# Three attention output projections as 64-row pairs at the end of the gate/up stage

## The chip, the cores and the metric

The kernel runs on one core of a Trainium2 chip. The metric is device time in microseconds (us), the median of the runs shown. The engines are TensorE (PE in the profile, with its weight loads as PEld), VectorE (DVE), ScalarE (ACT), GpSimd (POOL) and SyncE (SP); SyncE and GpSimd issue nearly all DMAs.

## The reference

One block with adaptive layer norm, 2048 rows of 576 channels, bf16: attention over a dilated window of 8 keys with 32 heads of 18 channels, then a gated bilinear feed-forward part with 4608 hidden channels. Cut to what matters:

```python
h = layernorm(x) * (1 + ca) + sa
qkv = h @ wqkv
o = windowed_attention(qkv)          # 8 keys, 2 apart, softmax
x = x + ga * (o @ wo)                # the output projection
h = layernorm(x) * (1 + cb) + sb
x = x + gb * (((h @ w_gate) * (h @ w_up)) @ w_down)
```

`sa, ca, ga, sb, cb, gb` come from `silu(c) @ w_mod`.

## The kernel before, in words

The rows are cut into 8 chunks of 256 (`CH`), each with two tiles of 128 rows. The feed-forward part takes the chunks in five groups, `GROUPS = [[0], [1, 2], [3, 4], [5, 6], [7]]`. For each group there is a stage `gate_up` (36 tiles of 128 hidden channels) and a stage `down` (the 36 tiles back to 576 channels).

576 channels are four tiles of 128 and a rest of 64. In gate/up a `Pair` computes two outputs at once, each half matmul using 64 of the 128 rows of TensorE: 9 steps of 64 channels, one output on the low rows and the other on the high rows, then swapped. `Pair.first` issues 10 of the 18 half matmuls, `Pair.second` the 8 others, and the first part of the next pair goes between. Gate and up of a tile are such a pair (`wg_pair`, 512 columns), and so are the q, k and v projections of later chunks (`qk_pair`, `v_pair`), which are put between the gate/up pairs. For that the last 64 rows of their weights stand twice in SBUF, in partitions 0 to 63 and 64 to 127, and so do the last 64 channels of their input.

All engines' orders are written out by the program at build time (manual schedule). `timed` is a small planner: it goes through the gate/up items, takes the next extra pair when its mark is due, and lets threads of other pieces (attention of the next group's chunks, layer norms, DMAs) in when its estimate of VectorE's time allows. A piece is `(TensorE time, VectorE time, needs, mark, wait, call)`; the times are the author's estimates in us, and they fix the order alone: on the chip every instruction waits for its data by semaphores. `among` does the same with the items of a down stage.

Attention of the chunks of the next group runs during gate/up, mostly on VectorE: products (`b_p`), logits (`b_l`, transposed by DMA in `b_ltd`), softmax (`b_sm0`, `b_sm1`), values (`b_mul`, `b_add`). The value windows `vsh` (1152 KB for one 128-row tile) are loaded by GpSimd (`b_ld`) into two buffers. The last `b_add` of a tile writes the attention output `o_sb`, rows by channels, 640 wide, of which 64 are padding with zeros. `b_od` issues two transposed DMAs on SyncE (one for each 128 rows) from `o_sb` to `oT`, channels by rows. `o_sb` and `oT` exist once.

`b_w` is the output projection of 128 rows: 5 matmuls of 64 columns (`pwr`) and 5 of 512 (`pw`) over five tiles of channels with 128 rows each (the last one padded with zeros), then three VectorE instructions that multiply with `ga` and add the residual `x_r`, giving a tile of `x1`. Chunk 0 has a form of its own. For every other chunk, `b_w` runs among the matmuls of the down stage of the group before. In a down stage of groups 1 to 3, `out_of` makes a thread for the next group's first chunk: `b_w` twice, the second layer norm (`b_ln`, `b_norm`), its transposes (`b_td`) into `h2T`, and the modulation (`b_mod`); the second chunk's thread begins with its `b_od` after the first chunk's `x1`. For the first chunk `b_od` was issued during gate/up before.

Loads of gate and up weights (`wgu`, two times 512 KB for four tiles) are issued by SyncE into three buffers, those of the down weights (`wd`, 576 KB) by GpSimd; some go to spaces free at that time (`prod_t`, `vsh`, `hh`).

Of the kernel before, what the change touches and what calls it, by code (L numbers as in the profile page):

```python
# [39 lines left out]
GC = D // 4  # L40

GROUPS = [[0], [1, 2], [3, 4], [5, 6], [7]]


@with_exitstack
def kernel(
# [48 lines left out]
    def js(j):  # L95
        return slice(j * P, (j + 1) * P)
# [44 lines left out]
    def load_res(i):  # L141
        x_res[i] = xres.tile([P, ST, D], BF, name="x_r")
        nc.sync.dma_start(x_res[i][:], x_rows(i))
# [399 lines left out]
    def b_mul(i, j, w0, n=2):  # L543
# [2 lines left out]
        at = b["attn"][:, j, w0:w0 + n, None, :].to_broadcast([P, n, DH, H])  # L546
        nc.vector.tensor_tensor(v, v, at, ALU.mult)  # L547

    def b_add(i, j, s):
        b = bb[i]  # L550
        vsh = b["vsh"][j]
        if s < 2:
            d = slice(2 * s, 2 * s + 2)
            nc.vector.tensor_tensor(vsh[:, d], vsh[:, d], vsh[:, 4 + 2 * s:6 + 2 * s], ALU.add)
        else:
            nc.vector.tensor_tensor(vsh[:, 0:2], vsh[:, 0:2], vsh[:, 2:4], ALU.add)
            nc.vector.tensor_tensor(o_sb[:, j, 0:D].rearrange("p (d h) -> p d h", d=DH), vsh[:, 0], vsh[:, 1], ALU.add)  # L557

    def b_o(i):
        pA = ps([P, 4, CH], BF, "oT_pA")  # L560
# [77 lines left out]
    def b_od(i):  # L638
        for j in range(ST):
            nc.sync.dma_start_transpose(out=oT[:, :, js(j)], in_=o_sb[:, j, :])  # L640
# [18 lines left out]
    def b_norm(i):  # L659
        bb[i]["rsq"]()  # L660
        bb[i]["norm"]()
# [24 lines left out]
    def prods_of(i):  # L686
        r = []
        if i >= 3:
            r = [(0, 0.82, "", f"p{i}{v}", 1.0, lambda v=v: b_p(i, v)) for v in range(W)]
            return r + [(1.3, 0, f"p{i}7", f"l{i}", 1.2, lambda: b_l(i, 0, 2)), (0, 0, f"l{i}", f"t{i}4", 9.0 if i == 7 else 6.0, lambda: [b_ltd(i, w) for w in (0, 4)])]  # L690
        for w in (0, 4):
            r += [(0, 0.82, "", f"p{i}{v}", 1.0, lambda v=v: b_p(i, v)) for v in range(w, w + 4)]
            r += [(0.75, 0, f"p{i}{w + 3}", f"l{i}{w}", 1.0, lambda w=w: b_l(i, w)), (0, 0, f"l{i}{w}", f"t{i}{w}", 9.0 if i == 7 else 6.0, lambda w=w: b_ltd(i, w))]
        return r

    def softmax_of(i):
        b1 = lambda: b_sm1(i)
        if i in GROUPS[1]:
            def total():
                b = bb[i]  # L700
                ssum = small.tile([P, ST, H], F32, name="ssum")
                nc.vector.tensor_reduce(ssum[:], b["dd"][:].rearrange("p j w h -> p j h w"), axis=AX.X, op=ALU.add)
                nc.scalar.activation(ssum[:], ssum[:], ACTF.Ln)
                b["rs"] = small.tile([P, ST, H], F32, name="rs")
                nc.scalar.activation(b["rs"][:], ssum[:], ACTF.Exp, scale=-1.0)

            def shares():
                b = bb[i]
                b["attn"] = attnp.tile([P, ST, W, H], BF, name="attn")
                nc.vector.tensor_tensor(b["attn"][:], b.pop("dd")[:], b.pop("rs")[:, :, None, :].to_broadcast([P, ST, W, H]), ALU.mult)  # L710
            return [(0, 1.4, f"t{i}4", "y1", 0.0, lambda: b_sm0(i, False)) if i == 1 else (0, 1.4, f"t{i}4", f"s{i}", 1.1, lambda: b_sm0(i)), (0, 1.05, f"s{i}", f"r{i}", 0.9, total), (0, 0.72, f"r{i}", f"a{i}", 0.0, shares)]
        return [(0, 1.4, f"t{i}4", f"s{i}", 1.1, lambda: b_sm0(i)), (0, 2.4, f"s{i}", f"a{i}", 0.0, b1)]

    def values_of(i, nxt=None):
        r = []
        for j in range(ST):
            r += [(0, 0.75, f"a{i}", "-", 0, lambda j=j, w=w: b_mul(i, j, w)) for w in range(0, W, 2)]
            r += [(0, 0.75, "", "-", 0, lambda j=j: b_add(i, j, 0)), (0, 0.75, "", "-", 0, lambda j=j: b_add(i, j, 1)),
                  (0, 1.2, "", f"o{i}{j}", 0, lambda j=j: b_add(i, j, 2))]
            if nxt is not None:  # L720
                r.append((0, 0, f"v{nxt}", "-", 0, lambda j=j: b_ld(nxt, j)))
        return r

    def attention_of(c1, c2):
        p2, sm = prods_of(c2), softmax_of(c1)
        if c1 < 3:
            first = prods_of(c1) + p2[:4] + sm[:1] + p2[4:6] + sm[1:] + p2[6:]
        else:
            first = prods_of(c1) + p2[:4] + sm + p2[4:]
        return first + values_of(c1, c2) + [(0, 0, "", "-", 0, lambda: b_od(c1))] + softmax_of(c2) + values_of(c2)  # L730

    def norm_of(n, after, free, load=None):
        def go():
# [12 lines left out]
    def qkv_of(n, free):  # L746
        r = []
        for k, ms in enumerate(QKP):
            r.append((0.98 if len(ms) == 2 else 0.52, f"h{n} {free}", f"q{n}{k}",
                      lambda ms=ms, k=k: (a_halo(n) if k == 0 else None, qk_pair(n, ms))[1]))  # L750
        return r + [(1.1, f"h{n}", f"w{n}", lambda: v_pair(n, 0)), (1.1, f"h{n}", f"v{n}", lambda: v_pair(n, 1))]
# [84 lines left out]
    def v_pair(i, hf):  # L836
# [16 lines left out]
                    nc.gpsimd.dma_start(vd[r0:r0 + P, :], v_sb[:].rearrange("p d h -> p (d h)"))  # L853
        return Pair(("pv", "pv"), D // 2, (side(0), side(1)), finish)

    QKP = [(0, 1), (2, 3), (4,), (5, 6), (7, 8)]

    def timed(items, extra, threads, slack, busy=0.0):

        t, dve = 0.0, busy  # L860
        done, seq = {f"v{i}": 0.0 for g in GROUPS for i in g[1:]}, []
        done["late"] = 0.0
        extra, threads = list(extra), [list(th) for th in threads]

        def ready(need):
            return all(done.get(x, 1e9) <= t for x in need.split())

        def fill():
            nonlocal t, dve
            moved = True  # L870
            while moved:
                moved = False
                for th in threads:
                    if th and ready(th[0][2]) and (not th[0][1] or dve <= t + slack):
                        pe, d, _, mark, wait, call = th.pop(0)
                        t += pe
                        dve = max(dve, t) + d if d else dve
                        done[mark] = (dve if d else t) + wait
                        seq.append(("piece", call))
                        moved = True  # L880
                        break
        for kind, f, step, own, need in items:
            if seq and extra and ready(extra[0][1]):
                pe, _, mark, make = extra.pop(0)
                seq.append(("pair", make))
                t += pe
                done[mark] = t + pe + 1.0
                fill()
            assert ready(need), (need, t)
            seq.append((kind, f))  # L890
            fill()
            dve = max(dve, t) + own
            t += step
        assert not extra, (extra[0][1], t)
        return seq, [(*p[0:2], p[2] if all(x in names(th) for x in p[2].split()) else "late", *p[3:]) for th in threads for p in th]
# [387 lines left out]
    def loads_v(i):  # L1283
        for j in range(ST):
            b_ld(i, j)
# [28 lines left out]
    def gb_row():  # L1314
# [17 lines left out]
                                         (0, 0, "r4", "e4", 2.0, lambda: aa[4]["norm"]((0,))), (0, 0, "e4", "n4", 1.6, lambda: aa[4]["norm"]((1,))),  # L1332
                                         (0, 0, "n4 v3", "x4", 0, nop)],
               first, [(0, 0, "y1", "s1", 0.6, lambda: b_exp(1))]]),
           1: (qkv_of(5, "p37"),
               [[(0, 0, "", "-", 0, lambda: (loads_v(3), load_res(3), load_res(4)))], norm_of(5, "p33", "", 7), second]),
           2: (qkv_of(6, ""),
               [[(0, 0, "", "h6", 1.0, lambda: (loads_v(5), load_res(5), load_res(6)))], attention_of(5, 6)]),
           3: (qkv_of(7, ""), [[(0, 0, "", "h7", 1.0, lambda: load_res(7)), (0, 0, "v7", "-", 0, lambda: loads_v(7))], [(0, 0, "q74", "-", 0, nop)] + prods_of(7) + softmax_of(7) + values_of(7) + [(0, 0, "", "-", 0, lambda: b_od(7))]]),
           4: ([], [])}  # L1340

    def first_down(late):
# [13 lines left out]
              (0, 2.2, "", "s2", 0.7, lambda: b_ln(2)), (0, 1.5, "s2", "n2", 0.2, lambda: b_norm(2)), (0.55, 1.0, "n2", "-", 0, lambda: b_t(2))]  # L1356
        return [a4, out_1(True), late + [(0, 0, "", "a2", 0.0, nop)] + values_of(2) + o2, [q(0), q(1), q(2), q(3), q(4), v(0), v(1)]]

    def out_of(i, first):
        r = [(0, 0, "", f"o{i}", 3.0, nop) if first else (0, 0, f"x{i - 1}", f"o{i}", 6.5, lambda: b_od(i))]  # L1360
        return r + [(1.2, 1.35, f"o{i}", "-", 0, lambda: b_w(i, 0)), (1.2, 1.35, "", f"x{i}", 0.5, lambda: b_w(i, 1)),
                    (0, 2.3, "", f"s{i}", 0.7, lambda: b_ln(i)), (0, 1.5, f"s{i}", f"n{i}", 0.2, lambda: b_norm(i)),
                    (0, 0, f"n{i}", f"t{i}", 6.5, lambda: b_td(i)),
                    (0, 1.0, f"t{i}", "-", 0, lambda: (b_mod(i, (3, 4), False), b_mod(i, (0, 1, 2), True)))]

    def next_down(gi, late):
        c1, *c2 = GROUPS[gi + 1]
        norm = norm_of(5 + gi, "", "") if gi < 3 else []
        return [late + out_of(c1, True)] + [out_of(c, False) for c in c2] + [norm]

    left = []
    for gi, grp in enumerate(GROUPS):
# [48 lines left out]
```

## Time and profile before

| | |
|---|---|
| median of 3 runs | 540.39 us (540.39 to 541.31) |
| the profiled execution | 540.11 us, span 538.4 us |
| mean granted TensorE clock | 0.998 |
| TensorE / VectorE / ScalarE / GpSimd busy | 99% / 59% / 47% / 13% |
| gate/up of chunks 1 and 2 | ends at 205.6 us |
| the down stage after it | 205.6 to 245.9 us |

The span goes from the first instruction to the last. Busy shares are averages over stages. A matmul's listed duration holds its way through the array: successive matmuls overlap, and what one costs is the distance of the starts. A DMA's line gives the time of its issue; "to landing" is from issue to its semaphore.

### The profile page before, as it was taken

How to read it: one execution, taken by the hardware profiler on the slowest of the kernel's cores; microseconds unless marked ns; L12 is line 12 of the kernel's file. 1: busy time of each engine (PE TensorE's matmuls, PEld its weight loads, DVE VectorE, ACT ScalarE, POOL GpSimd, SP SyncE). 2: the span in 40 equal slices, each digit the busy share in tenths (PEclk: the TensorE clock that was granted, in tenths of full speed). 3: DMA queues.
4: the chain of work that ended last, by engine and by line, in shares of the span. 5: the costliest groups of instructions: out<-in, count | busy, mean ns of one | idle time of the engine just before them, and what ended most of it. 6: DMA issues, size and time to landing. Idle time of an engine off the chain costs nothing.

```text
span 538.4 us, 14603 instructions
## 1 busy us (share of the span) xinstructions
PE 532.1 (99%) x6196; PEld 319.7 (59%) x6196; DVE 316.7 (59%) x715; ACT 252.6 (47%) x620; POOL 70.7 (13%) x110
## 2 busy tenths in 40 slices
PE   8999999999999999999999999999999999999997
PEld 4787888657756444555544444555544445568875
DVE  5898787858766678627467786523517724032212
ACT  4866886634566552113655552104556550006630
POOL 8104013212000210111000010110010101110210
PEclk9999999999999999999999999999999999999999
DMA  9999999989853896979354952973395682759641
GB/s 284 298 268 344 344 280 312 337 171 325 282 131 96 265 192 151 224 225 303 95 170 126 307 190 69 237 216 109 104 297 176 170 280 81 233 145 298 226 118 38
DMA packets 94978, 114.67 MB, mean 213 GB/s; under 512 B 28001, under 2 KB 83698, under 8 KB 94786
## 3 DMA queue, kind: packets, MB, share of 16 engines
q1 hardware_dynamic: 83184, 67.14, 45.3%
q0 software_dynamic: 11424, 46.40, 28.1%
q8 instruction: 48, 0.79, 0.6%
q10 hardware_dynamic: 306, 0.21, 0.1%
q14 instruction: 16, 0.13, 0.1%
HBM read 103.29 MB, written 4.74 MB: 201 GB/s over the span
## 4 chain that ended last, share of the span: by engine, by line
PE 97%; DMA 1%; DVE 0%; SPq 0%; ACT 0%; issue 0%
PE pg L756 29%; PE pu L756 23%; PE acc L971 20%; PE pq L441 4%; PE pq L756 3%; PE pw L648 3%; PE accr L976 3%; PE acc L1026 3%; PE pv L756 2%; PE pv L464 2%; PE lgT L498 2%; DMA wmA<-in_w_mod_dram 1%; PE po L603 1%; PE pwj L625 0%; PE pwr L646 0%; PE accr L1029 0%
## 5 line engine op out<-in xcount | busy, mean ns | idle before, releaser
L756 PE MATMUL pg<-h2T,wgu 64*128 64x512 bf16 (+1 forms) x1376 | 265.4, 331 | 0.0
L756 PE MATMUL pu<-h2T,wgu 64*128 64x512 bf16 (+1 forms) x1376 | 264.6, 331 | 0.0
L756 PEld LDWEIGHTS <-wgu 64*128 64x128 bf16 x2752 | 133.9, 94 | 96.2
L807 ACT CAST u_sb<-pu 128x512 bf16<-128x512 f32 (+1 forms) x172 | 85.6, 497 | 141.4 <-PE pg L756 141.1
L810 DVE TENSOR_TENSOR hh<-g_sb,u_sb 128x512 bf16<-128x512 bf16 x136 | 57.5, 423 | 114.5 <-ACT g_sb L808 113.8
L808 ACT CAST g_sb<-pg 128x512 bf16<-128x512 f32 (+1 forms) x172 | 86.7, 504 | 0.0
L971 PE MATMUL acc<-wd,hh 128*128 128x512 bf16 x344 | 86.4, 380 | 0.0
L971 PEld LDWEIGHTS <-hh 128*128 128x128 bf16 x504 | 49.0, 98 | 59.3 <-issue 1.5
L976 PE MATMUL accr<-wd,hh 128*128 128x64 bf16 x344 | 62.4, 193 | 0.0
L756 PE MATMUL pu<-h2T,wgr 64*128 64x512 bf16 (+1 forms) x188 | 61.4, 327 | 0.0
L756 PE MATMUL pg<-h2T,wgr 64*128 64x512 bf16 (+1 forms) x188 | 61.4, 327 | 0.0
L976 PEld LDWEIGHTS <-hh 128*128 128x128 bf16 x504 | 45.8, 98 | 1.9
L174 POOL DMA_DIRECT2D wd<-in_B_w_down_dram x29 | 21.9, 754 | 178.3 <-PE accr L976 95.3
L547 DVE TENSOR_TENSOR vsh<-vsh,attn 128x1152 bf16<-128x1152 bf16 x56 | 39.8, 751 | 1.1 <-DMA vsh<-vd 1.1
L486 DVE TENSOR_TENSOR prod_t<-qT,kT 128x1280 bf16<-128x1280 bf16 x36 | 28.2, 818 | 3.5 <-ACT kT L827 2.7
L971 PE MATMUL acc<-prod_t,hh 128*128 128x512 bf16 x112 | 28.8, 380 | 0.0
L756 PEld LDWEIGHTS <-wgr 64*128 64x128 bf16 x376 | 18.5, 94 | 15.6 <-issue 2.3
L324 ACT ACTIVATE h2T<-h2T,modc 128x256 bf16<-128x256 bf16 x12 | 6.6, 592 | 42.1 <-DMA h2T<-xn 42.1
L480 POOL DMA_DIRECT2D vsh<-vd x14 | 12.6, 899 | 91.4 <-DVE o_sb L557 81.3
L441 PE MATMUL pq<-hT,wqk 128*128 128x256 bf16 (+1 forms) x225 | 21.7, 251 | 0.1
L756 PE MATMUL pq<-hT,wqk 64*128 64x256 bf16 (+1 forms) x360 | 21.6, 258 | 0.0
L976 PE MATMUL accr<-prod_t,hh 128*128 128x64 bf16 x112 | 21.6, 193 | 0.0
(216 smaller groups left out, 622.3 us busy)
## 6 DMA issues: line engine op xcount, KB each, us to landing
wgu<-in_B_w_gate_dram SPq DMA_DIRECT2D x41, 512.0 KB, 6.0
wgu<-in_B_w_up_dram SPq DMA_DIRECT2D x41, 512.0 KB, 7.7
wd<-in_B_w_down_dram POOLq DMA_DIRECT2D x29, 576.0 KB, 5.4
vsh<-vd POOLq DMA_DIRECT2D x14, 1152.0 KB, 9.3
prod_t<-in_B_w_down_dram POOLq DMA_DIRECT2D x8, 576.0 KB, 8.3
hh<-in_B_w_down_dram POOLq DMA_DIRECT2D x6, 576.0 KB, 7.5
x_t<-in_A_x_dram SPq DMA_DIRECT2D x8, 288.0 KB, 7.6
x_r<-in_A_x_dram SPq DMA_DIRECT2D x8, 288.0 KB, 9.2
```

The source lines that it names most:

```text
L174: return nc.gpsimd.dma_start(wb[:], B_w_down[r0:r0 + FB * P, :].rearrange("(k p) n -> p k n", p=P))
L441: nc.tensor.matmul(pq[:, gi, :], lhsT=wqk[:, kt, m * P:(m + 1) * P], rhs=hT[:, kt, cols], start=(kt == order[0] and not (by_k and gi)), st ...
L486: nc.vector.tensor_tensor(prod, aa[i]["qT"][:], aa[i]["kT"][:, :, off:off + CH], ALU.mult)
L547: nc.vector.tensor_tensor(v, v, at, ALU.mult)
L648: nc.tensor.matmul(pw[:], lhsT=oT[:, m, js(j)], rhs=wo[:, m, 0:512], start=(m == 0), stop=(m == KT - 1))
L756: return nc.tensor.matmul(out, lhsT=lhs, rhs=rhs, start=first, stop=last, skip_group_check=True)
L807: nc.scalar.copy(u[:, c, :], pu)
L808: nc.scalar.copy(g[:, c, :], pg)
L810: return lambda: nc.vector.tensor_tensor(hh[:, f - c:f + 1, :], g, u, ALU.mult)
L971: nc.tensor.matmul(acc[j][:], lhsT=hh[:, f, js(j)], rhs=wb[:, f % FB, 0:512], start=(f == 0), stop=(f == FT - 1))
L976: nc.tensor.matmul(accr[:, j, :], lhsT=hh[:, f, js(j)], rhs=wb[:, f % FB, 512:D], start=(f == 0 and j == 0), stop=(f == FT - 1), skip_grou ...
L1026: nc.tensor.matmul(acc[i][:], lhsT=hh[:, f, js(j)], rhs=wb(f)[:, c0:c1], start=(f == 0), stop=(f == FT - 1))
```

## The change

For chunks 3, 5 and 7 (`PAIRED`), the first chunks of groups 2, 3 and 4, the output projection is made by two pairs (`w_pair`, 288 columns each, one side for each 128 rows) near the end of the gate/up stage in which their attention runs. `b_w` stays for the other chunks.

So that both halves of TensorE's rows hold the last 64 channels, `wo_both` copies the last 64 rows of `wo` to the upper partitions (GpSimd, once, at the start of the gate/up stage of chunks 1 and 2), and `o_tail` writes the last two channels of all heads (64 columns) of the attention output a second time, into the padding of `o_sb`; for chunks 4 and 6 it writes zeros there instead, since `b_w` runs over all 128 rows.

The pairs' results are multiplied with `ga` and get the residual in eight VectorE instructions a chunk. In the planner, `b_od` of the paired chunks gets a mark `O3`, `O5`, `O7`, due 14 us (11 us for chunk 7) after its place, and the pairs need it. In the down stages, the paired chunks have their layer norm, transposes and modulation left (`norm2_of`), and the thread of chunk 4 or 6 (`out_of`) begins with its `b_od` at the start of the stage.

In the order of the engines: on TensorE, the first pair stands five gate/up tiles before the end of the stage, the second one tile later. On SyncE, the transposes of chunk 4 (and 6) to `oT` come ahead of the first weight load of the next gate/up stage, where they came behind it, and the second layer norm's transposes of chunk 3 (and 5) ahead of those of the next chunk to be normalised.

```diff
+PAIRED = (3, 5, 7)
...
+    def o_tail(i, j):
+        d = o_sb[:, j, D:]
+        if i not in PAIRED:
+            nc.vector.memset(d, 0.0)
+            return
+        vsh = bb[i]["vsh"][j]
+        nc.vector.tensor_tensor(d.rearrange("p (d h) -> p d h", h=H), vsh[:, 0, DH - 2:], vsh[:, 1, DH - 2:], ALU.add)
...
             nc.vector.tensor_tensor(o_sb[:, j, 0:D].rearrange("p (d h) -> p d h", d=DH), vsh[:, 0], vsh[:, 1], ALU.add)
+            if i >= PAIRED[0]:
+                o_tail(i, j)
...
-        return first + values_of(c1, c2) + [(0, 0, "", "-", 0, lambda: b_od(c1))] + softmax_of(c2) + values_of(c2)
+        return first + values_of(c1, c2) + [(0, 0, "", f"O{c1}", 14.0, lambda: b_od(c1))] + softmax_of(c2) + values_of(c2)
...
+    def wo_both():
+        nc.gpsimd.tensor_copy(wo[64:, KF, :], wo[0:64, KF, :])
+
+    def w_pair(i, hf):
+        cs = slice(hf * D // 2, (hf + 1) * D // 2)
+        if hf == 0:
+            x1[i] = [x1p.tile([P, D], BF, name="x1") for _ in range(ST)]
+
+        def side(j):
+            return lambda rows, k: (oT[rows, k, js(j)], wo[rows, k, cs])
+
+        def finish(*outs):
+            for xt, o in zip(x1[i], outs):
+                nc.vector.tensor_tensor(xt[:, cs], o, ga_bc[:, cs], ALU.mult)
+            for j, xt in enumerate(x1[i]):
+                nc.vector.tensor_tensor(xt[:, cs], xt[:, cs], x_res[i][:, j, cs], ALU.add)
+        return Pair(("pw", "pw"), D // 2, (side(0), side(1)), finish)
+
+    def wo_of(i):
+        return [(1.1, f"O{i}", f"W{i}{hf}", lambda hf=hf: w_pair(i, hf), 1.15) for hf in range(2)]
...
-           1: (qkv_of(5, "p37"),
+           1: (qkv_of(5, "p37") + wo_of(3),
...
-           2: (qkv_of(6, ""),
+           2: (qkv_of(6, "") + wo_of(5),
...
+           3: (qkv_of(7, "") + wo_of(7), ...
...
-    def out_of(i, first):
-        r = [(0, 0, "", f"o{i}", 3.0, nop) if first else (0, 0, f"x{i - 1}", f"o{i}", 6.5, lambda: b_od(i))]
...
+    def out_of(i):
+        return [(0, 0, "", f"o{i}", 6.5, lambda: b_od(i)), (1.2, 1.35, f"o{i}", "-", 0, lambda: b_w(i, 0)),
+                (1.2, 1.35, "", f"x{i}", 0.5, lambda: b_w(i, 1))] + norm2_of(i, "")
...
-        return [late + out_of(c1, True)] + [out_of(c, False) for c in c2] + [norm]
+        return [late + [p for c in c2 for p in out_of(c)], norm2_of(c1, ""), norm]
```

More of the change, by code (lines that the diff above doesn't have):

```diff
@@ L883, in timed @@
             if seq and extra and ready(extra[0][1]):
-                pe, _, mark, make = extra.pop(0)
+                pe, _, mark, make, *ve = extra.pop(0)
                 seq.append(("pair", make))
                 t += pe
+                dve = max(dve, t) + sum(ve)
                 done[mark] = t + pe + 1.0
@@ L1334 @@
                first, [(0, 0, "y1", "s1", 0.6, lambda: b_exp(1))]]),
-           1: (qkv_of(5, "p37"),
-               [[(0, 0, "", "-", 0, lambda: (loads_v(3), load_res(3), load_res(4)))], norm_of(5, "p33", "", 7), second]),
-           2: (qkv_of(6, ""),
+           1: (qkv_of(5, "p37") + wo_of(3),
+               [[(0, 0, "", "-", 0, lambda: (loads_v(3), load_res(3), load_res(4), wo_both()))], norm_of(5, "p33", "", 7), second]),
+           2: (qkv_of(6, "") + wo_of(5),
                [[(0, 0, "", "h6", 1.0, lambda: (loads_v(5), load_res(5), load_res(6)))], attention_of(5, 6)]),
-           3: (qkv_of(7, ""), [[(0, 0, "", "h7", 1.0, lambda: load_res(7)), (0, 0, "v7", "-", 0, lambda: loads_v(7))], [(0, 0, "q74", "-", 0, nop)] + prods_of(7) + softmax_of(7) + values_of(7) + [(0, 0, "", "-", 0, lambda: b_od(7))]]),
+           3: (qkv_of(7, "") + wo_of(7), [[(0, 0, "", "h7", 1.0, lambda: load_res(7)), (0, 0, "v7", "-", 0, lambda: loads_v(7))], [(0, 0, "q74", "-", 0, nop)] + prods_of(7) + softmax_of(7) + values_of(7) + [(0, 0, "", "O7", 11.0, lambda: b_od(7))]]),
            4: ([], [])}
@@ L1357, in first_down, with norm2_of @@
         return [a4, out_1(True), late + [(0, 0, "", "a2", 0.0, nop)] + values_of(2) + o2, [q(0), q(1), q(2), q(3), q(4), v(0), v(1)]]
-    def out_of(i, first):
-        r = [(0, 0, "", f"o{i}", 3.0, nop) if first else (0, 0, f"x{i - 1}", f"o{i}", 6.5, lambda: b_od(i))]
[L1361 to L1364, printed above, removed]
+    def norm2_of(i, need):
+        return [(0, 2.3, need, f"s{i}", 0.7, lambda: b_ln(i)), (0, 1.5, f"s{i}", f"n{i}", 0.2, lambda: b_norm(i)),
+                (0, 0, f"n{i}", f"t{i}", 6.5, lambda: b_td(i)),
+                (0, 1.0, f"t{i}", "-", 0, lambda: (b_mod(i, (3, 4), False), b_mod(i, (0, 1, 2), True)))]
+    def out_of(i):
+        return [(0, 0, "", f"o{i}", 6.5, lambda: b_od(i)), (1.2, 1.35, f"o{i}", "-", 0, lambda: b_w(i, 0)),
+                (1.2, 1.35, "", f"x{i}", 0.5, lambda: b_w(i, 1))] + norm2_of(i, "")
     def next_down(gi, late):
```

## The prediction

> **What bounds the kernel now.** I read the page first: busy shares, then the chain that ended last.
>
> ```profile
> PE 532.1 (99%) x6196; PEld 319.7 (59%) x6196; DVE 316.7 (59%) x715; ACT 252.6 (47%) x620; POOL 70.7 (13%) x110
> PE 97%; DMA 1%; DVE 0%; SPq 0%; ACT 0%; issue 0%
> ```
>
> TensorE is the path: from about 11 us to 533 us it never waits for anything worth naming. So a change is worth the TensorE time it takes away, minus every wait that it puts in front of TensorE. Both are read below; the profiled execution took 540.11 us (span 538.4 and 1.7 around it), 0.28 below the median of 540.39.
>
> **What TensorE saves.** The timeline of TensorE shows one old half projection (`b_w`, one 128-row tile of chunk 5), and the chain in order of time shows one pair of exactly the new form (18 half matmuls, 288 columns, a value pair of chunk 7):
>
> ```profile
> 329.07 0.31 PE L646 MATMUL pwr<-wo,oT 128*128 128x64 bf16 x5
> 329.22 1.24 PE L648 MATMUL pw<-wo,oT 128*128 128x512 bf16 x5
> 330.30 0.38 PE L971 MATMUL acc<-wd,hh 128*128 128x512 bf16 x1
> ...
> 383.38 1.10 PE pv L756 x18
> ```
>
> From 329.07 to 330.30 one `b_w` holds TensorE 1.23 us, a chunk 2.46. A pair takes 1.10 to 1.11, a chunk two of them, 2.21. Three chunks: 3 x 0.25 = 0.7 us saved, 0.13% of the time. A measurement of this kernel can tell about 0.2% (1.1 us) from no change, so by itself this would hardly be seen.
>
> **When the pairs' operand is there.** Each pair reads oT for both halves of the chunk: its first matmul needs the first transposed DMA, its second the second. Before, `b_w` read oT in the down stage, long after. In the new order the first pair of chunk 3 stands directly ahead of the first pg matmul of a gate/up item that the timeline of TensorE has here:
>
> ```profile
> 194.89 0.38 PE L756 MATMUL pg<-h2T,wgr 64*128 64x512 bf16 x1
> ```
>
> Nothing ahead of that place is added to TensorE, so it gets there at 194.9. SyncE's timeline, GpSimd's, and the oT instructions of that window (issue to landing) say when oT is there:
>
> ```profile
> 183.46 0.37 SPq L157 DMA_DIRECT2D wgu<-in_B_w_gate_dram  x1
> 183.88 0.50 SPq L157 DMA_DIRECT2D wgu<-in_B_w_up_dram  x1
> 184.47 2.80 SPq L640 DMA_TRANSPOSE oT<-o_sb  x2
> ...
> 184.89 0.91 POOL L480 DMA_DIRECT2D vsh<-vd  x1 [4.78 <-DVE o_sb L557]
> 190.15 1.52 POOL L174 DMA_DIRECT2D prod_t<-in_B_w_down_dram  x2 [4.36 <-DMA wgu<-in_B_w_up_dram]
> ...
> DMA to landing us min/median/max: 15.8/17.2/18.5
> ```
>
> The two transposes, issued at 184.5 and 185.8, land at 200.3 and 204.3. The first landing has a witness in VectorE's timeline, which stood still for it before overwriting o_sb:
>
> ```profile
> 200.39 0.46 DVE L557 TENSOR_TENSOR o_sb<-vsh 128x576 bf16<-128x576 bf16 x1 [2.18 <-DMA oT<-o_sb]
> ```
>
> The reason for 15 to 18 us, where the transposes of chunk 7 take 2.6 and 5.4, is the company: two weight loads of 512 KB directly ahead in SyncE's queue, then the 1152 KB vsh load and two 576 KB prod_t loads. From the table of stretches (length, then busy time of PE, PEld, DVE, ACT and POOL, granted clock, share of the DMA engines' time, GB/s):
>
> ```profile
> 189.00:194.00 5.00, 5.00 (x50) 2.24 (x46) 4.13 (x8) 3.00 (x6) 1.52 (x2) 1.00 1.05 77
> 194.00:202.00 8.00, 8.00 (x76) 3.60 (x74) 5.78 (x12) 4.51 (x9) 0.00 (x0) 1.00 1.10 268
> ```
>
> In the first of these five us the DMA engines are wholly busy (1.05) and move 77 GB/s, against 268 afterwards: transposes and the vsh load in each other's way. None of these issues waits for the pair, so the change keeps the collision. `o_tail` (two 64-element additions; the nearest row, 64 wide on VectorE, is 185 ns) makes the vsh load and, at most, the second transpose about 0.2 us later; that does not take them apart. Price: 204.3 - 194.9 = **9.4 us of idle TensorE**. Bounds: 6 us if the second transpose lands like the first with the small shift (201), 11.5 if it lands 2 us later. I take the row's own 9.4.
>
> **The clock after the wait.** An idle stretch of that length is nowhere inside the trace, but its two ends bound what follows. At the start seven 512-column matmuls take 3.12 us, the next six (one half as wide) 1.36; and after the last matmul the mean granted clock falls (0.81 in the stretch, same columns):
>
> ```profile
> 1.27 3.12 PE L202 MATMUL busy<-busy_w 128*128 128x512 bf16 x7 [1.27 <-DVE busy_w L197]
> 4.62 1.36 PE L202 MATMUL busy<-busy_w 128*128 128x512 bf16 x6
> ...
> 534.00:538.40 4.40, 0.63 (x6) 0.32 (x4) 1.35 (x5) 0.00 (x0) 0.00 (x0) 0.81 0.20 67
> ```
>
> So TensorE begins at half speed for some 3 us, losing 1.5; and 0.81 over 4.4 us means full speed for 2.7 us and half for 1.7, so it fell about 3.5 us after the last matmul. A wait of 9.4 us is longer than that: I add 1.5 us (bounds 0, if the clock holds, and 1.7). The Trainium skill (TensorE: Matmul & The Clock Gate, The HAM clock gate) has a window of about 3.4 us idle to fall and as much busy work to rise, which would make it an estimated 1.7 in place of 1.5; the trace's own 3 and 3.5 us agree with that as far as they go.
>
> **What else moves, and its cover.**
> - VectorE. Per chunk two `b_w` ends (223 + 692 + 458 ns each, 2.75 us) become four multiplications of 288 from PSUM (about 0.46, between the 223 ns of 64 and the 692 of 512) and four additions (about 0.30, between 185 and 417): 3.0 us, plus 0.4 for `o_tail`. In gate/up of chunks 1 and 2 the multiplications stand ahead of the last values of chunk 4, so those wait for the pair too. By rows they then need 7 us after the second pair's end: o_sb of chunk 4 at about 220.6, with the stage's end moved from 205.6 to 218.9. Before it was 207.4: the same 1.7 behind. Nothing on TensorE there waits.
> - SyncE. Chunk 4's (and 6's) transposes now stand ahead of the first weight load of the next gate/up, which so goes out near 222 instead of 191.2. It took up to 17.7 us then and is first read at 245.9 (moved to about 256.6): covered by over 15 us. Without that cover it would cost its landing time. Transposes issued by 222 with landings of 3 to 5 us are there for `b_w` of chunk 4, which comes 8 us into the down stage, at 227 and 229. Margin 2 to 4 us, so 0 (at worst 2).
> - GpSimd. One copy of 64x576 (a memset of that size took 573 ns) after the vsh loads at 126.4; GpSimd then idles until 176.0, and the first reader is the pair. 0.
> - Down stages. Layer norm of chunks 3, 5 and 7 starts with the stage instead of after two `b_w`: earlier, and h2T was early already (landings by 236 for a read at 245.9). 0.
> - Chunks 5 and 7: their pairs stand at 310.6 and 434.7 on the old time axis. Chunk 7's oT lands by 428.6. Chunk 5's first transpose lands at 304.1, the second (issued at 299.9) is not recorded; with the first's 7.8 us it is there at 307.7, 3 us early. 0, but see the rivals.
>
> **Sum on the profiled execution:** 540.11 - 0.7 + 9.4 + 1.5 = 550.3 us; with the 0.28 of the median, **550.6 us**.
>
> **Rivals.**
> 1. *The transposes get through in time.* If chunk 3's oT lands within 10.4 us of its issue instead of 15.8 and 18.5, no wait arises and 0.7 us are left: 539.7, inside 0.2%. For it: 10 transposes of oT have a median of 5.2 us, and a start of the vsh load 2 us later would leave them alone, as at chunk 5, where it was issued after them. Against: all issues involved keep their order and nearly their time. Chance 0.13. With 0.4 us more from work that now overlaps better it would be faster than 0.2%, 539.2: no row points there; 0.05.
> 2. *A short wait.* The transposes land between 196 and 201: 1 to 6 us, with less or no clock loss: 541 to 546, say 543.5. 0.08.
> 3. *Chunk 5 too.* There also a 1152 KB vsh load is issued at 300.2, right behind the second transpose. With 18.5 us to landing that one would come at 318.4, 7.8 us after its pair's place: about 6 to 9 us with the clock, 557. Against: the trace has 7.8 us for the first. 0.06.
> 4. *The pair's halves do not overlap*, so the change is no saving at all: 18 matmuls of 288 columns one after the other take 2.2 us, a chunk 4.4, three chunks 5.8 us more than before beside the wait: 557. Against: the value pair above has the same form and takes 1.10. 0.02.
>
> **How the numbers follow.** The forecast with the wait and the slow clock has 0.66; its own range is 546 (landing at 201, clock held) to 553 (206, with 1.7). 542 to 557 adds most of rivals 2 and 3 and the fourth: about 0.80. Faster by over 0.2%: 0.05. Within: 0.13. Slower: 0.66 + 0.08 + 0.06 + 0.02 = 0.82.
>
> **What would show it.** In the changed profile: an idle stretch of TensorE ahead of the first pw of chunk 3, put down to DMA oT<-o_sb, about 9 us long, near 195; a digit of the clock line below 9 right after it; pairs of 1.10 us; no idle time ahead of the pw of chunks 5 and 7; the stage ends after 205 all later by the same amount. It would be wrong if oT's issue to landing there were under 10 us, or if the time grew without such a gap.

## The result and the profile after

The changed kernel is slower: median 548.25 us of 22 runs against 540.80 of 22 runs of the kernel before, 7.45 us or 1.4% more. Its runs scatter from 539.54 to 552.54, those of the kernel before from 539.89 to 542.65. The ratio measured for the two kernels is 1.0076 (95% interval 1.0055 to 1.0098); it leaves out runs over 1.5% above a kernel's fastest, which here are 13 of the changed kernel's 22, the profiled one among them, so it understates the loss and the medians of all runs stand beside the ratios below.

The profiled execution took 548.91 us, span 547.1. Its page has the new state in the shares and in the chain that ended last:

```profile
PE 533.7 (98%) x6214; PEld 328.9 (60%) x6244; DVE 317.2 (58%) x731; ACT 252.6 (46%) x620; POOL 71.1 (13%) x111
...
PE 86%; DMA 11%; DVE 1%; issue 1%; ACT 0%; SPq 0%; ACTq 0%
```

The chain now leaves TensorE: it goes through DMAs, `oT<-o_sb` among them with 2.6% (a load in the start phase, `hh<-in_B_w_up_dram`, has 3.7%). The changed kernel's TensorE timeline has the place (the bracket is the idle time just before, and what ended it):

```profile
197.34 0.38 PE L767 MATMUL pg<-h2T,wgu 64*128 64x512 bf16 x1
200.64 0.29 PE L767 MATMUL pw<-wo,oT 64*128 64x288 bf16 x1 [2.92 <-DMA oT<-o_sb]
202.64 0.87 PE L767 MATMUL pw<-wo,oT 64*128 64x288 bf16 x8 [1.71 <-DMA oT<-o_sb]
```

TensorE is free at 197.55 (starts of these half matmuls are 0.21 apart); the first half matmul of the pair waits for the first transpose, the second for the other. From 197.55 to 202.64 are 5.1 us. The oT instructions of that window, issue to landing:

```profile
L651 SPq DMA_TRANSPOSE oT<-o_sb x2: 1199/1265/1331, 187.1 to 188.4; - x2
...
DMA to landing us min/median/max: 13.5/13.8/14.2
```

And two stretches, during the wait and just after it (columns as in the prediction):

```profile
197.60:202.60 5.00, 0.41 (x3) 0.09 (x1) 2.48 (x5) 1.07 (x2) 0.00 (x0) 1.00 0.66 231
202.97:206.38 3.41, 3.41 (x22) 2.34 (x20) 0.02 (x1) 1.07 (x2) 0.00 (x0) 0.50 0.04 14
```

TensorE resumes at half clock for 3.41 us, which loses 1.7. The 8.7 us between the two spans add up: 2.8 were there long before the pair (the tile that starts at 78.82 before starts at 81.59), 5.1 wait, 1.7 clock, less 0.7 for three chunks, 8.9. The 2.8 build up in small steps: 0.8 up to the tile that starts at 47.90 before, most of the rest between 61 and 82 us, where the chain has passed through a load of `hh` that took 20.1 us to land. The three traces of the kernel before lie within 0.5 us of each other at the transposes and show no such lag, but e1_no3 below does, behind an `hh` load of 20.3 us, and its median has no loss; the timed runs of the kernel before scatter by 2.8 us too. That the change has no part in the 2.8 is not shown.

### The profile page after: what moved, and what is told of

The parts are those of the page before. It is cut to its first block, busy times and chain, and to the rows that moved or that the text cites. A ratio compares the mean times of both kernels' runs of the same rounds, so it can differ in the third digit from the quotient of the medians.

```text
span 547.1 us, 14691 instructions
## 1 busy us (share of the span) xinstructions
PE 533.7 (98%) x6214; PEld 328.9 (60%) x6244; DVE 317.2 (58%) x731; ACT 252.6 (46%) x620; POOL 71.1 (13%) x111
## 4 chain that ended last, share of the span: by engine, by line
PE 86%; DMA 11%; DVE 1%; issue 1%; ACT 0%; SPq 0%; ACTq 0%
PE pg L767 26%; PE pu L767 21%; PE acc L1004 19%; DMA hh<-in_B_w_up_dram 4%; PE pq L767 3%; PE accr L1009 3%; DMA oT<-o_sb 3%; PE acc L1059 3%; DMA v_e<-vd 2%; PE pq L442 2%; PE pv L767 2%; PE pw L659 2%; PE pw L767 1%; DMA wmA<-in_w_mod_dram 1%; PE lgT L499 1%; DMA vd<-v_sb 1%
## 5 line engine op out<-in xcount | busy, mean ns | idle before, releaser
L767 PEld LDWEIGHTS <-wgu 64*128 64x128 bf16 x2752 | 141.5, 94 | 90.6 <-DMA wgu<-in_B_w_up_dram 0.2
L1004 PE MATMUL acc<-wd,hh 128*128 128x512 bf16 x327 | 84.0, 380 | 0.1
L767 PEld LDWEIGHTS <-wgr 64*128 64x128 bf16 x376 | 20.9, 94 | 14.9 <-issue 2.7
L1004 PE MATMUL acc<-prod_t,hh 128*128 128x512 bf16 x108 | 27.7, 380 | 0.0
L767 PE MATMUL pq<-hT,wqk 64*128 64x256 bf16 (+1 forms) x360 | 23.0, 259 | 0.0
```

The costliest lines, as they stand in the source:

```text
L767: return nc.tensor.matmul(out, lhsT=lhs, rhs=rhs, start=first, stop=last, skip_group_check=True)
L1004: nc.tensor.matmul(acc[j][:], lhsT=hh[:, f, js(j)], rhs=wb[:, f % FB, 0:512], start=(f == 0), stop=(f == FT - 1))
```

## The experiments

All times are medians of all runs; the kernel before ran on the same chip and had 541.5, 541.6 and 540.7 us in the three sets. Ratios come with their 95% intervals. The diffs are cut to the lines that matter. The expectations weigh three accounts. Theory A is TensorE's wait for oT with the slow clock after it, theory B a cost of each pair by itself, and rival C transposes made late by what stands ahead of them in SyncE's own queue.

**Which chunk costs it.** Experiment e1_no3 takes chunk 3 alone back to `b_w`, e2_only3 keeps chunk 3 alone.

```diff
# e1_no3
-PAIRED = (3, 5, 7)
+PAIRED = (5, 7)
-           1: (qkv_of(5, "p37") + wo_of(3),
+           1: (qkv_of(5, "p37"),
# e2_only3
+PAIRED = (3,)      # and no wo_of(5), wo_of(7)
# both: unpaired first chunks get their b_w thread of the kernel before
```

> Chunks 5 and 7 keep their pairs, chunk 3 goes back to two b_w in the down stage (its last 64 attention channels are not doubled; wo stays doubled). Theory A (all of the loss is TensorE's wait for chunk 3's oT, with the slow clock after it): the loss is gone, 2 x 0.25 us saved, so 0.1% below the kernel before (540.3 against 540.8), no idle stretch of TensorE over 1 us behind the start phase, no half clock inside. Theory B (each pair costs by itself: VectorE frees its banks late, the queues moved on SyncE and VectorE): two thirds of the loss stay, about +5 us.

> Only chunk 3 has its pairs; chunks 5 and 7 go back to b_w. Theory A: the whole loss is here, and scatters as in the changed kernel: median 545 to 551, an idle stretch ahead of the first pw pair of 4 to 10 us, then half clock for about 3.4 us. Theory B: a third of the loss, about +2.5 us, in every run alike.

e1_no3: 541.93 us of 10 runs, 1.0007 (0.999 to 1.0025): the loss is gone, the 0.1% of gain can't be told from nothing. e2_only3: 549.96 of 4 runs, 545.50 to 552.16, 1.0149 (1.0096 to 1.0203): all of the loss, and its scatter, sits in chunk 3's pairs. Its TensorE timeline has the gap again, with a shorter wait than in the changed kernel's profile:

```profile
194.42 0.28 PE L767 MATMUL pw<-wo,oT 64*128 64x288 bf16 x1
197.90 0.42 PE L767 MATMUL pw<-wo,oT 64*128 64x288 bf16 x2 [3.20 <-DMA oT<-o_sb]
```

Here only the second transpose was late. Theory B (each pair costs something) falls: the pairs of chunks 5 and 7 cost nothing that can be measured, those of chunk 3 everything.

**Is the wait landing less arrival, and is the collision its cause?** e3_vsh_behind leaves the pair where it is and moves the DMAs beside it; e4_late leaves all DMAs and moves the pair.

```diff
# e3_vsh_behind: values_of(3, 4) without its last piece, then
+            ld = (0, 0, f"v{c2}", "-", 0, lambda: behind(b_ld(c2, 1), bb[c1]["od"]))   # od: the second transpose
+            return first + v[:-1] + [od, ld] + softmax_of(c2) + values_of(c2)
# e4_late
-    f"O{c1}", 14.0,
+    f"O{c1}", 20.0 if c1 == 3 else 14.0,
```

> The changed kernel, with one DMA moved: the 1152 KB vsh load of chunk 4's second tile waits for the landing of chunk 3's oT transposes (and the two prod_t loads behind it in GpSimd's queue with it). Theory A with the collision as its cause: the transposes land 5 to 8 us after their issue, by 193, ahead of TensorE's arrival at 195; no wait; the vsh load lands near 202, just when VectorE wants it; 539.7 to 540.3, 0.1 to 0.2% below the kernel before. Rival C (the transposes are late by what stands ahead of them in SyncE's own queue, not by the vsh load): they still land 14 us or more after their issue, and the wait stays.

> The changed kernel, with chunk 3's pairs three gate/up tiles (5.8 us) later, at the very end of the stage; all DMAs as they were. Theory A: the wait is landing less arrival, so it shrinks by up to 5.8 us: TensorE arrives near 200.7 and waits 0 to 4 us, mostly too short for the clock to fall; median 540 to 543. Theory B: no change from the changed kernel, 548.

e3_vsh_behind: 541.10 us of 10 runs, 0.9986 (0.997 to 1.0002); the expected 539.7 to 540.3 was missed, with the kernel before at 541.5 on this chip. The transposes' lines and TensorE's timeline:

```profile
L651 SPq DMA_TRANSPOSE oT<-o_sb x2: 1199/1263/1327, 187.3 to 188.6; - x2
...
DMA to landing us min/median/max: 4.4/4.8/5.2
```

```profile
197.53 0.38 PE L772 MATMUL pg<-h2T,wgu 64*128 64x512 bf16 x1
197.74 0.78 PE L772 MATMUL pw<-wo,oT 64*128 64x288 bf16 x10
198.35 0.38 PE L772 MATMUL pu<-h2T,wgu 64*128 64x512 bf16 x1
```

With the same two weight loads ahead of them in SyncE's queue, the transposes now land in 5.2 and 4.4 us, and the pair starts 0.21 us after the matmul before it. So rival C, the queue ahead, falls; what makes them late is the traffic beside them. A second trace of this version (e5_vsh_behind_5 below) has 5.0 and 4.2 us, and of its 22 timed runs in all none took more than 543.17.

e4_late: 542.30 us of 10 runs, 1.0003 (0.9981 to 1.0024). The transposes landed 11.3 and 15.9 us after their issue, yet the wait was short, because TensorE came 5.8 us later:

```profile
202.94 0.28 PE L767 MATMUL pw<-wo,oT 64*128 64x288 bf16 x1
203.91 0.78 PE L767 MATMUL pw<-wo,oT 64*128 64x288 bf16 x9 [0.69 <-DMA oT<-o_sb]
```

At the old place that execution would have waited 6.8 us (landing at 203.9, arrival at 197.1). So the loss goes with the reader's place as well as with the traffic.

**Which load, and is anything gained without the wait?** e6_prod_behind makes the two prod_t loads alone wait for the transposes. e5_vsh_behind_5 is e3_vsh_behind again with more runs, the version that should beat both kernels.

```diff
# e6_prod_behind, in ld_prods
-                behind(r, wgu_in[gi * NBLK + NBLK - 1])
+                behind(r, bb[3]["od"] if gi == 1 else wgu_in[gi * NBLK + NBLK - 1])
```

> The changed kernel, with the two 576 KB prod_t loads alone waiting for the landing of chunk 3's oT; the 1152 KB vsh load stays where it was. If all bytes beside the transposes count alike, half of the delay goes: oT lands about 10 us after its issue instead of 13 to 18, the wait is 0 to 3 us, median 541 to 544. If the vsh load alone is the cause: landing and wait as in the changed kernel, median 546 to 550.

> The kernel whose vsh load of chunk 4 waits for chunk 3's oT, again and more often. Theory A: with no wait left only the 0.7 us that TensorE saves remain, ratio 0.9987 to the kernel before (0.998 to 0.9995). Rival: nothing is saved, ratio 1.000, because the pairs' VectorE work and the moved queues cost as much.

e6_prod_behind: 543.16 us of 10 runs (539.86 to 548.41), 1.0016 (0.9992 to 1.004). The transposes landed 10.6 and 11.4 us after their issue, and TensorE's timeline has short waits at the pair:

```profile
200.17 0.29 PE L767 MATMUL pw<-wo,oT 64*128 64x288 bf16 x1 [0.84 <-DMA oT<-o_sb]
200.73 0.78 PE L767 MATMUL pw<-wo,oT 64*128 64x288 bf16 x9 [0.27 <-DMA oT<-o_sb]
```

The median lies where the first expectation has it (541 to 544), the landings a little above its 10 us. In these single executions the prod_t loads give about 3 of the 9 us of delay (13.8 down to 11.0) and the vsh load the other 6 (down to 4.8), though their sizes are equal (1152 KB); with landings that scatter as shown below, the shares are no more than indicated.

e5_vsh_behind_5: 541.46 us of 12 runs against 541.59, 0.999 (0.9966 to 1.0014). Both measurements of this version have a ratio just below 1 and intervals that hold 1: it takes back the loss, and a gain over the kernel before is not shown by the times. TensorE's timeline shows it by stages: see the first point of the next section.

**How far the wait scatters.** Two more profiles of each kernel (e7 and e11 of the changed one, e8 and e12 of the kernel before), and e9_load_first, in which the next weight load is again issued beside the transposes, as before the change.

```diff
# e9_load_first, in out_of: the transposes of chunk 4 only after the stage's first load
-        return [(0, 0, "", f"o{i}", 6.5, lambda: b_od(i)), ...
+        return [(0, 0, "", f"w{i}x", 1.5, nop), (0, 0, f"w{i}x", f"o{i}", 6.5, lambda: b_od(i)), ...
```

> The changed kernel once more, to see how far the wait itself scatters: TensorE's arrival at the first pair of chunk 3 stays 10.4 us behind the issue of the first transpose, the second lands 14 to 20 us after that issue, and the idle stretch is the difference, 3 to 9 us; half clock for 3.4 us after it; span 544 to 550.

> The kernel before once more: if 19.8 us from the first issue to the second landing was an outlier of the profiled execution, it is 14 to 17 us here, which makes the wait of the forecast 4 to 7 us instead of 9.4; if it is the rule, 18 us or more.

> The changed kernel once more, for the scatter: arrival 10.4 us behind the first transpose's issue; second landing 14 to 18 us behind it; the idle stretch is the difference.

> The kernel before once more, for the scatter: 16 to 20 us from the first issue to the second landing, with the weight load issued at 6.7 us.

> The changed kernel, with chunk 4's transposes to oT a little later in the order, so that the next weight load (wgu, two times 512 KB) is again issued about 6.7 us after chunk 3's transposes, as in the kernel before, and competes with them. If that load, which the change had moved away, makes the difference between 18.5 to 19.8 us (two profiles of the kernel before, from the first transpose's issue to the second's landing) and 14.7 to 15.5 (two of the changed kernel): 18 us or more here, a wait of 7 to 9 us, median 550 to 552. If it does not matter: 14 to 17 us and a median of 547 to 549, as in the changed kernel.

From the first transpose's issue to the second's landing, and the wait (TensorE's arrival at the pair's place lies 10.4 us behind that issue):

| profile | issue to landing, us | wait, us |
|---|---|---|
| before, first / e8 / e12 | 19.8 / 18.5 / 9.5 | none (read later); would be 9.4 / 8.1 / 0 |
| changed, first / e7 / e11 | 15.5 / 14.7 / 14.9 | 5.1 / 4.3 / 4.5 |
| e1_no3 | 16.1 | none (read later); would be 5.7 |
| e9_load_first | 15.9 | 5.5 |
| e2_only3 | 13.9 | 3.5 |
| e4_late | 17.2 | 0.8 (pair later); would be 6.8 |
| e10_warm (below) | 16.8 | 2.1 (matmuls put in); would be 6.4 |
| e6_prod_behind | 11.9 | 1.5 |
| e3_vsh_behind, e5_vsh_behind_5 | 5.7, 5.5 | 0 |

e7_after_look and e11_after_look (548.71 and 546.26 us) came out as expected. e9_load_first: 548.11 us of 7 runs, 542.93 to 553.13, 1.0111 (1.0072 to 1.0151): as the changed kernel, so the moved weight load makes no difference that these runs can tell. e8_before_look (540.55 us) stands with the long ones, e12_before_look (540.42 us) contradicts what I expected of it (16 to 20). The landings of their transposes, e8_before_look's first:

```profile
DMA to landing us min/median/max: 13.6/15.4/17.2
```

```profile
DMA to landing us min/median/max: 7.3/7.8/8.2
```

The stretch of e12_before_look, and the same stretch of the first profile of the kernel before, which the issues reach at the same times within 0.3 us:

```profile
188.00:196.00 8.00, 8.00 (x77) 3.62 (x74) 6.36 (x12) 4.58 (x10) 1.51 (x2) 1.00 1.11 326
```

```profile
188.00:196.00 8.00, 8.00 (x78) 3.62 (x76) 6.65 (x12) 4.58 (x9) 1.52 (x2) 1.00 1.12 154
```

The first is e12_before_look's: the DMA engines as busy, 326 GB/s. In the second they moved 154. The same DMAs at the same times sometimes get in each other's way and sometimes do not. The two longest landings, 19.8 and 18.5, are both of the kernel before and above all of the changed kernel's; but the shortest is of the kernel before as well, so that the change itself shortens them is neither shown nor excluded.

**The clock term by itself.** e10_warm puts matmuls without use into the wait.

```diff
+        if hf == 0 and i == 3:
+            bank = ps([P, NB], F32, "busy")
+            for _ in range(18):
+                nc.tensor.matmul(bank[:], lhsT=shifts[:, 0:P], rhs=wgr[:, 0:NB], start=True, stop=True)
```

> The changed kernel, with 18 matmuls of 512 columns on idle data (3.8 us) between TensorE's arrival and chunk 3's first pair; their result is not used. Theory A with its clock term: the wait that is left is 1 to 4 us, mostly too short for the clock to fall; full clock behind it, so 1.7 us less than the changed kernel in the median, 546 to 547. Without a clock term (the half clock costs nothing): the median of the changed kernel, 548 to 549. If the pairs never waited, 3.8 us more than the kernel before would stand: 545.

547.75 us of 4 runs (546.48 to 551.56), 1.0148 (1.0105 to 1.0191): inconclusive in the median. Its TensorE timeline says why:

```profile
195.85 3.62 PE L877 MATMUL busy<-wgr,shifts 128*128 128x512 bf16 x16
199.40 0.29 PE L767 MATMUL pw<-wo,oT 64*128 64x288 bf16 x1
201.75 0.78 PE L767 MATMUL pw<-wo,oT 64*128 64x288 bf16 x9 [2.06 <-DMA oT<-o_sb]
202.26 0.38 PE L767 MATMUL pu<-h2T,wgu 64*128 64x512 bf16 x1
...
202.86 0.63 PE L767 MATMUL pu<-h2T,wgu 64*128 64x512 bf16 x1
```

2.06 us of idle time were left, and the clock fell all the same, after TensorE had resumed: from 202.5 its 512-column matmuls take 0.63 in place of 0.38 for 3.4 us. Even this wait was too long, so the profiled run does not price the clock apart from the wait. Of the four runs two had a mean clock of 0.999 and 1.0 and took 546.48 and 547.48, about what was expected at full clock; the two at 0.997 took 548.03 (the profiled one) and 551.56. The first two have no trace, so their waits are not known.

## Why the prediction was right or wrong, point by point

- *What TensorE saves, 0.25 us a chunk: right.* The first matmuls of the gate/up stages of groups 2, 3 and 4, in TensorE's timeline of the kernel before and then of the changed one:

```profile
245.85 0.39 PE L756 MATMUL pg<-h2T,wgr 64*128 64x512 bf16 x1
365.43 0.39 PE L756 MATMUL pg<-h2T,wgr 64*128 64x512 bf16 x1
481.25 0.28 PE L756 MATMUL pg<-h2T,wgr 64*128 64x256 bf16 x1
```

```profile
255.05 0.39 PE L767 MATMUL pg<-h2T,wgr 64*128 64x512 bf16 x1
374.38 0.39 PE L767 MATMUL pg<-h2T,wgr 64*128 64x512 bf16 x1
489.96 0.28 PE L767 MATMUL pg<-h2T,wgr 64*128 64x256 bf16 x1
```

The lag goes from 9.20 to 8.95 to 8.71, so chunks 5 and 7 gave 0.25 and 0.24 us. In e5_vsh_behind_5, whose chunk 3 did not wait, the lag goes from 1.99 to 1.75 to 1.50; before the pair it was 2.23 (the first matmul of the stage in which the pair stands, 130.56 before, is at 132.79), so chunk 3 gave 0.24 there. That this would hardly be seen in the times was right too.
- *The wait for chunk 3's oT: mechanism and place right, size wrong.* The term "I take the row's own 9.4" failed. It was the longest of a scattering quantity, taken from one execution as if the trace were a constant: of three profiles of the kernel before the same subtraction gives 9.4, 8.1 and 0, and the waits measured in five executions with the pair at its place were 3.5 to 5.5. The bounds of 6 to 11.5 were drawn around that one row, and all five lie below them. With 5.1 and 1.7 the sum is 540.8 - 0.7 + 6.8 = 546.9, nearer to the 548.25 measured than 550.6; the 1.3 us between are not placed, since the timed runs have no trace. That the median still lies in the forecast's own range of 546 to 553 is in part luck, then. The fastest of the 22 timed runs, 539.54 at full clock, is close to the 539.7 of rival 1 (only the savings are left), though no trace shows that it did not wait; the longest is 552.54.
- *The clock after the wait: right that it falls; the price was 1.7 in the profiled execution, not 1.5.* The Trainium skill's window (TensorE: Matmul & The Clock Gate, The HAM clock gate) of about 3.4 us to rise is what the trace shows, 3.41 us. For the fall, my 3.5 us was a misreading: the stretch from 534.00 still has six matmuls in it, 0.63 us of TensorE's time, so the last ended near 534.6 and the fall at 536.7 came 2.1 us behind it. So that row did not agree with the Trainium skill's idle window of about 3.4 us either, and e10_warm does not: 2.06 us sufficed there, while 0.97 us between starts in e4_late left the clock at full. The measurements decide. Nor is there a fixed delay: the trace of e8_before_look ends 3.7 us after its last matmul with the clock still at 1.00. e9_load_first had the half clock for 6.83 us, twice 3.41. It fell at 199.36, inside the wait, while TensorE resumed only at 200.96:

```profile
199.36:200.96 1.60, 0.00 (x1) 0.01 (x2) 0.00 (x0) 0.00 (x0) 0.00 (x0) 0.50 0.96 266
200.96:206.18 5.22, 5.22 (x30) 3.52 (x32) 0.43 (x1) 1.07 (x2) 0.00 (x0) 0.50 0.39 125
```

So 5.22 us of work ran at half clock there, which loses 2.6; the part inside the wait costs nothing. The mean clock of the 22 timed runs hints at how often each came: one stretch of 3.41 us lowers the mean by 1.7 of 547, or 0.0031, and the runs show 1.0 twice, 0.997 ten times (median 546.3), 0.994 nine times (548.6) and 0.991 once (552.5). By that, most runs had one or two stretches and lost 1.7 to 3.4 us, against the 1.5 of my sum.
- *The collision as cause: right.* e3_vsh_behind shows it by taking it apart, twice with e5_vsh_behind_5. That the issues keep their order was right; that the collision then always comes about as it did was an assumption, and e12_before_look shows an execution in which it did not.
- *VectorE, SyncE, GpSimd: right.* Multiplications 452 ns (0.46 said), `o_tail` 183 ns, the copy 679 ns in GpSimd's idle time. Chunk 4's o_sb was done at 220.0, 2.8 us behind the stage's end at 217.2 (1.7 said); the weight load went out at 221.3 (222 said); and `b_w` of chunk 4 began without a wait.
- *Chunks 5 and 7: right.* No idle time ahead of their pairs; rival 3 did not come about. Rival 4 neither: pairs take 1.1 us.

What stays open: why the same DMAs, issued at the same times, land after 9.5 us in one execution and 19.8 in another, how the waits are distributed over the 22 timed runs, which have no trace, what sets the moment at which the clock falls, and why one idle stretch is followed by one half-clock stretch in some executions and by two in others.

## What to carry to other kernels

Moving the reader of a DMA forward turns a landing time that nobody waited for into a wait, so price it from the landing and not from the issue, and from several executions: a duration that hides behind slack is not controlled by anything, and one trace is one draw. Where it must be early, take the traffic beside it away (here one dependency brought 15.5 us down to 5.7, from the first issue to the second landing) or let the reader come later. With a TensorE wait of 2 us and more, reckon with a clock that falls after it as well: here every wait of 3.5 us and more brought one, and so did one of 2.06.

## What the runs showed of the hardware that was not expected

- TensorE's clock fell to half after an idle stretch of only 2.06 us (e10_warm) and stayed there for 3.41 us; after 0.97 us it did not (e4_late). In e9_load_first it stayed for 6.83 us.
- The delay of that fall is not fixed: at the end of the trace it came 2.1 us after the last matmul in one execution of the kernel before, and in another (e8_before_look) it had not come after 3.7 us.
- Over the same 8 us, with the same transposes and loads in flight, the DMA engines moved 154 GB/s in one execution and 326 in another, and were over 100% busy by their own account in both (1.12 and 1.11). Their busy share does not tell what they move.
